# A decode step on one Trainium2 core: W_Q in four transfers of 16, 16, 32 and 64 rows instead of one of 128

## The chip, the cores and the metric

The kernel runs on one core of a Trainium2 chip. The metric is device time in microseconds from the start to the end of one execution. Before the change it is 196.24 us, the median of three runs (196.23 to 196.3).

## What is computed

The program is one decode step, for a batch of four with one token each, of a block in which attention and a gated feed-forward run in parallel on the same normalised input:

```python
x  = A_x                                   # 4 x 1 x 512, bf16
xn = _layernorm(x)
# A: 32 query heads, 8 KV heads, head size 128, only the last W = 4096 positions
q = xn @ wq                                # 512 x 4096
scores = einsum("bhqd,bhkd->bhqk", q, k) * Dh ** -0.5
o = einsum("bhqk,bhkd->bhqd", softmax(scores), v) @ wo     # wo is 4096 x 512
# B: gated feed-forward, F = 1792
ffn = (silu(xn @ w_gate) * (xn @ w_up)) @ w_down
return x + o + ffn
```

Keys and values are 33.5 MB each, W_Q and W_O 4 MB each, the three feed-forward matrices 1.8 MB each: 81 MB are read for a 4 KB result.

## The kernel before

Work is staged by KV head: eight passes, one for each head, over blocks of 4 MB of keys and 4 MB of values. A block has 128 partitions (the rows of on-chip memory), each with one contiguous run of 32 KB. There are two buffers for keys (KB) and two for values (VB). In a pass TensorE transposes the 128 key tiles (L416), VectorE and ScalarE copy the transposes out of PSUM (L336, L267), TensorE forms the scores (L425), VectorE takes maxima (L340), ScalarE the exponentials (L270), and TensorE sums and multiplies with the values (L521, L434).

All large loads are issued by SyncE, on one queue, in an order written out by hand in `run_sync`: W_Q, W_gate, W_up, K0, K1, V0, then alternately a key and a value block as buffers come free, then W_down and W_O in five pieces of columns. A key load from the third on waits until the transposes of an earlier block are done; a value load from the second on waits until an earlier product with the values is done. The small input x is loaded by ScalarE's queue (L257).

W_Q has no buffer of its own. It lies in the second value buffer (`WQ`, L57), 128 rows of 32 KB: row p holds rows 4p to 4p+3 of the matrix. It is loaded once, by the first instruction of `run_sync` (L237), and announces itself on the semaphore of that buffer, `d_v[1]`, by 16. The buffer's next user, V1, is loaded after a product with the values has released it.

TensorE's head (`t_head`) transposes the normalised x, waits for `d_v[1]` to reach 16 (L469) and then runs 32 matmuls over W_Q (L473); each contracts over all 128 partitions. ScalarE and VectorE copy the result out (L261, L310), TensorE transposes it (L480), and then the gate and up products follow (L487). TensorE's first pass begins when K0 has landed.

In the pass for head r the product with the values belongs to the pass before. In the first pass it runs over what the second value buffer holds then, W_Q, with its result unused, and with that it releases the buffer.

Of the kernel before, what the change touches and what calls it, by code (L numbers as in the profile page):

```python
# [10 lines left out]
def bass_parallel_sum__sliding_block_cached__swiglu_ffn__decode_kernel(  # L11
# [45 lines left out]
    WQ = VB[1][:].rearrange("p t d -> p (t d)").rearrange("p (c n) -> p c n", c=NC)  # L57
# [66 lines left out]
    def sem(name):  # L124
        return nc.alloc_semaphore(name=name)

    d_x = sem("d_x")
    d_k = [sem("d_k%d" % g) for g in range(2)]
    d_v = [sem("d_v%d" % g) for g in range(2)]
    d_wg = sem("d_wg")  # L130
# [46 lines left out]
    wq_ap = A_wq.rearrange("(p c) n -> p c n", c=NC)  # L177
# [7 lines left out]
    def kv_ap(cache, r):  # L185
        return cache[:, r, Sk - W:, :].rearrange("b (s t) d -> s b (t d)", t=NT)
# [39 lines left out]
    def run_sync(eng):  # L226
        def load_k(r):
            if r >= 2:
                eng.wait_ge(s_tr[NCH - 1], r - 1)
            eng.dma_start(KB[r % 2][:].rearrange("p t d -> p (t d)"), kv_ap(A_k_cache, r)).then_inc(d_k[r % 2], 16)  # L230

        def load_v(r):
            if r:
                eng.wait_ge(s_pv, r)
            eng.dma_start(VB[r % 2][:].rearrange("p t d -> p (t d)"), kv_ap(A_v_cache, r)).then_inc(d_v[r % 2], 16)

        eng.dma_start(WQ[:], wq_ap).then_inc(d_v[1], 16)  # L237
        eng.dma_start(WG[:], wg_ap).then_inc(d_wg, 16)
        eng.dma_start(WU[:], wu_ap).then_inc(d_wu, 16)
        load_k(0)  # L240
        load_k(1)
        load_v(0)
        for r in range(2, HKV):
            load_k(r)
            load_v(r - 1)
        load_v(HKV - 1)
        eng.dma_start(WD, wd_ap).then_inc(d_wd, 16)
        for q, (a, b) in enumerate(ROWS):
            if q == 0:
                eng.wait_ge(s_tr[NCH - 1], HKV - 1)  # L250
            eng.dma_start(WO[:, a:b, :], wo_ap[:, a:b, :]).then_inc(d_wo[q], 16)
        eng.wait_ge(s_y, 2)
        eng.dma_start(out_ap, y[:]).then_inc(d_out, 16)
        eng.wait_ge(d_out, 16)
# [140 lines left out]
    def run_tensor(eng):  # L395
# [60 lines left out]
        with nc.body("t_head", valid_engines=me):  # L456
            loc = eng.mark_branch_hint_location()
            for t, v in ((nx, 1), (odd, 0), (nk[0], 16), (nk[1], 16)):
                nc.regs_mov(t, v)
            eng.wait_ge(s_c2, 1)  # L460
            eng.wait_ge(s_xn, 1)
            for c in range(NC):
                last = eng.transpose(xT_ps[:, c * B:(c + 1) * B],  # L463
                                     xn[:].rearrange("b (p c) -> b c p", c=NC)[:, c, :], ident[0:B, 0:B])
            last.then_inc(s_xT, 1)
            eng.wait_ge(s_const, 1)
            mm(mask_ps, Lsel[:], Dsh[:])
            eng.wait_ge(s_xnT, 1)
            eng.wait_ge(d_v[1], 16)  # L469
            for c in range(NC):  # L470
                for j in range(2):
                    for k in range(4):
                        last = mm(ps_S[j][32 * k:32 * k + 32, :], XnT[:, c, :],  # L473
                                  WQ[:, c, 512 * (4 * j + k):512 * (4 * j + k) + 512],
                                  start=(c == 0), stop=(c == NC - 1), skip_group_check=True)
            last.then_inc(s_q, 1)
            eng.wait_ge(s_qs, 2)
            for j in range(2):
                for h in range(4):
                    last = eng.transpose(qT_ps[:, 4 * j + h, :], qs[:, j, 128 * h:128 * h + 128], ident[:])  # L480
            last.then_inc(s_qt, 1)
            for w, d, o, s_w in ((WG, d_wg, gate_ps, s_g), (WU, d_wu, up_ps, s_u)):
                wt = w[:].rearrange("p c (m t) -> p c t m", t=NF)
                eng.wait_ge(d, 16)
                for c in range(NC):
                    for k in range(4):
                        last = mm(o[32 * k:32 * k + 32, :].rearrange("p (t m) -> p t m", m=128), XnT[:, c, :],  # L487
                                  wt[:, c, T0[k]:T0[k] + 4, :], start=(c == 0), stop=(c == NC - 1), skip_group_check=True)
                last.then_inc(s_w, 1)
            eng.wait_ge(s_gu, 1)  # L490
            for t in range(4):
                last = eng.transpose(gT_ps[:, t, :], gu[:, 128 * t:128 * t + 128], ident[:])
            last.then_inc(s_gt, 1)
            eng.wait_ge(s_qc, 1)
            eng.wait_ge(s_guT, 1)
            nc.br("t_pass", engines=me)
# [102 lines left out]

    run_gpsimd(nc.gpsimd)  # L600
    run_sync(nc.sync)
    run_scalar(nc.scalar)
    run_vector(nc.vector)
    run_tensor(nc.tensor)


# [26 lines left out]
```

## Time and profile before

| | |
|---|---|
| median of three runs | 196.24 us |
| the profiled execution's own time | 196.33 us |
| its span, first to last instruction | 195.0 us |
| granted TensorE clock, mean | 0.965 |
| TensorE matmul busy | 158.2 us (81%) |
| VectorE busy | 115.5 us (59%) |
| ScalarE busy | 69.2 us (35%) |
| DMA queue of SyncE and ScalarE: packets' share of 16 engines | 97.2% |
| HBM read | 81.01 MB, 415 GB/s over the span |
| W_Q, issue to landing | 12.3 us |
| a key block, issue to landing (median) | 26.3 us |

"Busy" is time in which an engine runs an instruction. The profile has a row of the DMA engines' busy share and of GB/s in forty equal slices of the span, 4.9 us each. In a view by stretches of time, a DMA packet is counted whole in the stretch in which it starts, so that a short stretch can show a share above 1.

### The profile page before, as it was taken

The numbers are of one execution on the slowest core, as the hardware profiler recorded it, in microseconds if no ns is written. First come the engines' busy times: TensorE is split into PE (matmuls) and PEld (weight loads), VectorE is DVE, ScalarE is ACT, GpSimd is POOL, SyncE is SP. The second block draws the span as 40 slices with busy tenths as digits, with TensorE's granted clock in tenths as the row PEclk, the third lists the DMA queues.
The fourth block names the chain that finished last, engine by engine and source line by source line (L and its number), as shares of the span: only waits on it lengthen the run. The fifth ranks groups of instructions, "written<-read, shape, count | busy, mean of one in ns | idle before, by whom it ended". The sixth has DMA issues, their size and how long they took to land.

```text
span 195.0 us, 6476 instructions
## 1 busy us (share of the span) xinstructions
PE 158.2 (81%) x2889; PEld 123.0 (63%) x2898; DVE 115.5 (59%) x220; ACT 69.2 (35%) x87; POOL 8.8 (5%) x26
## 2 busy tenths in 40 slices
PE   0038945998998899899989986998799849989994
PEld 0013105986787788778778865986588549866532
DVE  4832283667667586766758673667486717674402
ACT  2003100470664357056434704470466034704001
POOL 7910000000000000000000000000000000000000
PEclk9999995899999999999999999799999978999999
DMA  6999999999999999999999999999999999998991
GB/s 229 437 424 426 440 450 437 434 437 434 420 427 423 445 423 444 430 430 430 430 430 430 430 430 430 430 430 430 444 430 430 430 430 430 430 437 376 431 401 70
DMA packets 3621, 81.09 MB, mean 416 GB/s; under 512 B 408, under 2 KB 544, under 8 KB 928
## 3 DMA queue, kind: packets, MB, share of 16 engines
q1 hardware_dynamic: 3608, 81.01, 97.2%
q8 instruction: 4, 0.07, 0.1%
q14 instruction: 1, 0.01, 0.0%
q10 hardware_dynamic: 8, 0.00, 0.0%
HBM read 81.01 MB, written 0.00 MB: 415 GB/s over the span
## 4 chain that ended last, share of the span: by engine, by line
PE 43%; DMA 42%; ACT 8%; DVE 3%; issue 2%; SPq 1%; DVEq 0%; ACTq 0%
DMA kbuf<-in_A_k_cache_dram 42%; PE ps_kt L416 20%; PE ps_s L425 8%; ACT kT L267 7%; PE ps_o L434 5%; PE ps_kt L442 2%; PE ps_s L538 2%; DVE mxb L340 1%; ACT p L270 1%; PE ps_s L582 1%; PE ps_kt L525 1%; PE ps_o L542 1%; PE ps_s L593 1%; DVE mx L363 1%; PE ps_s L572 0%
## 5 line engine op out<-in xcount | busy, mean ns | idle before, releaser
L416 PE MATMUL ps_kt<-ident,kbuf 128*128 128x128 bf16 x1024 | 72.9, 229 | 11.9 <-DMA kbuf<-in_A_k_cache_dram 8.1
L416 PEld LDWEIGHTS ps_kt<-ident,kbuf 128*128 128x128 bf16 x1024 | 62.8, 103 | 18.9 <-DMA kbuf<-in_A_k_cache_dram 8.5
L336 DVE COPY kT<-ps_kt 128x1024 bf16<-128x1024 bf16 x80 | 52.3, 688 | 23.2 <-PE ps_kt L416 22.6
L267 ACT COPY kT<-ps_kt 128x1024 bf16<-128x1024 bf16 x48 | 47.8, 1013 | 47.4 <-PE ps_kt L416 47.4
L270 ACT ACTIVATE p<-ps_s 128x512 bf16<-128x512 f32 x32 | 16.5, 603 | 43.8 <-PE ps_s L538 43.8
L340 DVE TENSOR_REDUCE mxb<-ps_s 128x16 f32<-128x512 f32 x32 | 22.1, 692 | 13.2 <-PE ps_s L425 11.6
L425 PE MATMUL ps_s<-qT,kT 128*128 x1024 | 29.5, 170 | 0.0
L425 PEld LDWEIGHTS ps_s<-qT,kT 128*128 128x128 bf16 x1024 | 27.9, 96 | 0.3
L434 PE MATMUL ps_o<-vbuf,p 128*32 128x256 bf16 x576 | 17.4, 273 | 0.6
L434 PEld LDWEIGHTS ps_o<-vbuf,p 128*32 128x32 bf16 x576 | 15.0, 97 | 2.1 <-issue 1.8
L538 PE MATMUL ps_s<-dsh,lsel 128*128 128x512 bf16 x36 | 9.4, 382 | 0.0
L521 PE MATMUL ps_kt<-p,ones 128*128 128x512 bf16 x27 | 7.6, 379 | 0.9 <-ACT p L270 0.2
L473 PE MATMUL ps_s<-vbuf,xnT 128*32 128x512 bf16 x32 | 3.6, 629 | 5.5 <-DMA vbuf<-in_A_wq_dram 5.5
L344 DVE TENSOR_REDUCE dsum<-ps_kt 128x16 f32<-128x512 f32 x9 | 6.2, 692 | 1.5 <-PE ps_kt L521 1.3
L350 DVE TENSOR_TENSOR oT<-ps_o,rden 128x16 f32 (+1 forms) x9 | 1.6, 175 | 8.9 <-PE ps_o L542 8.9
L525 PEld LDWEIGHTS ps_kt<-identf,mxd 128*128 128x128 f32 x9 | 1.3, 139 | 8.4 <-DVEq L366 8.4
L525 PE MATMUL ps_kt<-identf,mxd 128*128 128x128 f32 x9 | 2.9, 323 | 4.5 <-DVEq L366 4.5
L542 PEld LDWEIGHTS ps_o<-fold,o 128*128 128x128 f32 x36 | 5.4, 191 | 1.3
L463 PE MATMUL ps_s<-ident,xn 4*128 4x4 bf16 x4 | 0.3, 166 | 7.1 <-DVE xn L298 7.1
L473 PEld LDWEIGHTS ps_s<-vbuf,xnT 128*32 128x32 bf16 x32 | 1.2, 138 | 7.0 <-issue 7.0
L538 PEld LDWEIGHTS ps_s<-dsh,lsel 128*128 128x128 bf16 x36 | 2.8, 97 | 4.1 <-issue 1.9
L273 ACT COPY part<-ps_s 64x512 f32<-64x512 f32 x1 | 0.6, 580 | 12.2 <-PE ps_s L582 12.2
(94 smaller groups left out, 81.2 us busy)
## 6 DMA issues: line engine op xcount, KB each, us to landing
kbuf<-in_A_k_cache_dram SPq DMA_DIRECT2D x8, 4096.0 KB, 26.3
vbuf<-in_A_v_cache_dram SPq DMA_DIRECT2D x8, 4096.0 KB, 28.4
vbuf<-in_A_wq_dram SPq DMA_DIRECT2D x1, 4096.0 KB, 12.3
kbuf<-in_A_wo_dram SPq DMA_DIRECT2D x1, 2048.0 KB, 31.3
wg_sb<-in_B_w_gate_dram SPq DMA_DIRECT2D x1, 1792.0 KB, 16.1
wu_sb<-in_B_w_up_dram SPq DMA_DIRECT2D x1, 1792.0 KB, 19.9
wg_sb<-in_B_w_down_dram SPq DMA_DIRECT2D x1, 1792.0 KB, 27.0
kbuf<-in_A_wo_dram SPq DMA_DIRECT2D x1, 896.0 KB, 34.4
```

Of the source, the lines that this page charges most:

```text
L267: eng.copy(KT[n % 8][:], kt_ps[n % 3]).then_inc(s_ev[n], 1)
L270: eng.activation(P[:, q * TB:(q + 1) * TB, :], S_ps[q], ACT.Exp, scale=SCALE).then_inc(s_xp[q], 1)
L336: eng.tensor_copy(KT[n % 8][:], kt_ps[n % 3]).then_inc(s_ev[n], 1)
L340: eng.tensor_reduce(mxb[:, q, :], S_ps[q].rearrange("p t c -> p c t"), AX.X, ALU.max)
L344: eng.tensor_reduce(dsum[:], dn_ps[:].rearrange("p (t c) -> p c t", c=CQ), AX.X, ALU.add)
L416: last = eng.transpose(kt_ps[n % 3][:, k, :], KB[g][:, 8 * n + k, :], ident[:])
L425: last = mm(S_ps[q][:, 8 * (n % 4) + k, :], KT[n % 8][:, k, :], QT[:, bass.ds(j, 1), :, :].rearrange("p o b h -> p (o b h)"), start=(n % 4 ...
L434: last = mm(o4_ps[32 * k:32 * k + 32, :], P[:, 2 * u:2 * u + 2, :].rearrange("p t c -> p (t c)"), VB[e][:, 2 * u:2 * u + 2, :].rearrange(" ...
L521: last = mm(dn_ps[:], ones[:], P[:, q * TB:(q + 1) * TB, :].rearrange("p t c -> p (t c)"), start=(q == 0), stop=(q == NB - 1))
L525: eng.transpose(mx_ps, mxd[:], identf[:]).then_inc(s_mt, 1)
L538: mm(S_ps[q], Lsel[:], bc(Dsh[:], TB), start=False, stop=True, skip_group_check=True).then_inc(s_sh[q], 1)
L542: last = mm(ot_ps, o4[:, 128 * e:128 * e + 128], fold[:, 16 * e:16 * e + 16], start=(e == 0), stop=(e == 1), skip_group_check=True)
```

## The change

W_Q's load becomes four loads of the same rows: rows 0 to 15, 16 to 31, 32 to 63 and 64 to 127, in this order, on the same queue and ahead of everything that was behind it. The first three announce themselves on a new semaphore, `d_wq`, by 16 each; the last one announces itself on `d_v[1]` as the whole did. TensorE waits for `d_wq` to reach 48 and then, as before, for `d_v[1]` to reach 16. Nothing else is changed.

```diff
     d_x = sem("d_x")
+    d_wq = sem("d_wq")
     d_k = [sem("d_k%d" % g) for g in range(2)]
...
-        eng.dma_start(WQ[:], wq_ap).then_inc(d_v[1], 16)
+
+        for a, b in ((0, 16), (16, 32), (32, 64), (64, 128)):
+            eng.dma_start(WQ[a:b], wq_ap[a:b]).then_inc(d_wq if b < 128 else d_v[1], 16)
         eng.dma_start(WG[:], wg_ap).then_inc(d_wg, 16)
...
             eng.wait_ge(s_xnT, 1)
+            eng.wait_ge(d_wq, 48)
             eng.wait_ge(d_v[1], 16)
             for c in range(NC):
```

## The prediction

> **What bounds the kernel now.** I read the page first: the head, the slices, the queues and the chain of waits.
>
> ```profile
> span 195.0 us, 6476 instructions
> ...
> DMA  6999999999999999999999999999999999998991
> GB/s 229 437 424 426 440 450 437 434 437 434 420 427 423 445 423 444 430 430 430 430 430 430 430 430 430 430 430 430 444 430 430 430 430 430 430 437 376 431 401 70
> ...
> q1 hardware_dynamic: 3608, 81.01, 97.2%
> ...
> DMA kbuf<-in_A_k_cache_dram 42%; PE ps_kt L416 20%; PE ps_s L425 8%; ACT kT L267 7%; PE ps_o L434 5%; PE ps_kt L442 2%; PE ps_s L538 2%; DVE mxb L340 1%; ACT p L270 1%; PE ps_s L582 1%; PE ps_kt L525 1%; PE ps_o L542 1%; PE ps_s L593 1%; DVE mx L363 1%; PE ps_s L572 0%
> ```
>
> The DMA engines are full from the second slice to the last but one. SyncE's one queue moves 81 MB and takes 97.2% of what sixteen engines have. The chain gives more of the span to compute than to DMA, but it prefers whatever instruction ran last. Long stretches say it better: the last two columns are the busy share of the sixteen DMA engines and GB/s.
>
> ```profile
> 0.00:1.76 1.76, 0.00 (x0) 0.00 (x0) 0.11 (x1) 0.43 (x1) 1.23 (x11) 1.00 0.01 2
> 1.76:12.65 10.89, 0.45 (x5) 0.31 (x5) 7.64 (x14) 1.06 (x2) 7.60 (x17) 1.00 1.00 406
> 12.65:51.70 39.05, 31.66 (x436) 20.28 (x438) 19.91 (x35) 10.50 (x13) 0.00 (x0) 0.91 1.02 436
> 51.70:120.00 68.30, 61.94 (x1304) 51.98 (x1305) 46.92 (x91) 32.16 (x40) 0.00 (x0) 1.00 1.00 429
> 120.00:192.40 72.40, 63.34 (x1136) 49.89 (x1142) 40.49 (x79) 24.70 (x31) 0.00 (x0) 0.95 0.98 419
> 192.40:195.00 2.60, 0.82 (x16) 0.51 (x10) 0.41 (x1) 0.36 (x1) 0.00 (x0) 1.00 0.01 2
> ```
>
> One unbroken stream, then, from 1.76 to 192.40 us, 2.6 us before the end. PE waits for it where a pass is short of work (chain of waits, start and duration), and the last matmuls wait for W_O's last row:
>
> ```profile
> 2.12 29.19 DMA kbuf<-in_A_k_cache_dram
> 94.89 25.30 DMA kbuf<-in_A_k_cache_dram
> 131.68 27.39 DMA kbuf<-in_A_k_cache_dram
> ...
> 191.86 1.11 PEld L593 LDWEIGHTS ps_s<-kbuf,oP 128*32 128x32 bf16 x20 [0.21 <-DMA kbuf<-in_A_wo_dram]
> ```
>
> K blocks that are issued at 94.89 and 131.68 land 25 to 27 us later because that much is queued ahead of them. So a microsecond that the stream loses at its head, where W_Q lies, is lost at the end; nothing behind it has slack to give back.
>
> **The change part by part.** The edited issue is the first on SyncE (timeline, start and duration):
>
> ```profile
> 0.73 0.57 ACTq L257 DMA_DIRECT2D x_sb<-in_A_x_dram  x1
> 0.73 0.41 SPq L237 DMA_DIRECT2D vbuf<-in_A_wq_dram  x1
> 1.20 0.41 SPq L238 DMA_DIRECT2D wg_sb<-in_B_w_gate_dram  x1
> 1.66 0.42 SPq L239 DMA_DIRECT2D wu_sb<-in_B_w_up_dram  x1
> ...
> 156.46 2.33 SPq L251 DMA_DIRECT2D kbuf<-in_A_wo_dram  x5
> ```
>
> *Issue.* A step of SyncE is 0.47 us (0.73 to 1.20; five W_O issues in 2.33), whatever the size. Three more make 1.41 us. W_gate, W_up, K0, K1 and V0 are issued that much later: W_gate at 2.61 instead of 1.20. The engines have W_Q to move until 12.65 at least, so this is hidden, by some 9 us. Without that cover it would cost 1.41.
>
> *The wait.* PE gets a wait for 48 on the new semaphore ahead of the old one. Queued behind it are the 32 Q matmuls, then gate and up; ScalarE and VectorE wait for those. The three early parts are queued ahead of the fourth, whose wait was there already, so it adds nothing but one satisfied wait. No part is used earlier than before: every Q matmul contracts over all 128 rows. And this prologue has room:
>
> ```profile
> 13.12 3.60 PE L473 MATMUL ps_s<-vbuf,xnT 128*32 128x512 bf16 x32 [5.50 <-DMA vbuf<-in_A_wq_dram]
> ...
> 29.27 0.18 DVE L329 COPY guT<-ps_kt 128x64 bf16<-128x64 bf16 x1
> 31.36 4.72 PEld L416 LDWEIGHTS ps_kt<-ident,kbuf 128*128 128x128 bf16 x46 [2.57 <-DMA kbuf<-in_A_k_cache_dram]
> ```
>
> It ends at 29.45, and PE then waits for K0. A late W_Q makes W_gate, W_up and K0 late by the same amount, so this order stays.
>
> *Completions.* Three more transfers end. Where W_gate follows W_Q the share below is 1.00 over 4.25 us; half of its last digit is 0.02 us for one seam. Three are 0.06 us at most; I take 0.06.
>
> *The move itself* decides. Rates again, cut where packets start: a window counts those that start in it.
>
> ```profile
> 1.76:2.61 0.85, 0.00 (x0) 0.00 (x0) 0.02 (x1) 0.85 (x1) 0.58 (x5) 1.00 2.14 618
> 2.61:3.60 0.99, 0.00 (x0) 0.00 (x0) 0.84 (x3) 0.01 (x1) 0.73 (x4) 1.00 0.00 0
> 3.60:4.20 0.60, 0.00 (x0) 0.00 (x0) 0.53 (x2) 0.00 (x0) 0.44 (x1) 1.00 2.05 874
> 4.20:12.10 7.90, 0.45 (x5) 0.31 (x5) 6.26 (x11) 0.20 (x1) 5.86 (x9) 1.00 0.92 398
> 12.10:16.35 4.25, 3.23 (x32) 1.24 (x32) 0.00 (x0) 0.00 (x0) 0.00 (x0) 1.00 1.00 428
> ```
>
> A row of W_Q is 32 KB, moved as one packet. 618 GB/s for 0.85 us is 0.525 MB, sixteen rows: the first round, one row for each engine, 2.14 x 0.85 x 16 / 16 = 1.82 us each. The next sixteen start from 3.60 on and take 1.23. The six rounds after that take 0.92 x 7.90 x 16 / 96 = 1.21 us a row, 27 GB/s for an engine. Eight rounds are 9.7 us.
>
> All of this is with transfers over 128 rows, where each engine feeds eight rows that no other engine feeds. After the change sixteen engines feed rows 0 to 15, then 16 to 31, then 32 to 63, then 64 to 127. Only one transfer in the trace has several engines feed neighbouring rows: x, four rows of 1 KB. Its first, second and fourth row (in the 1.74 window other packets are mixed in):
>
> ```profile
> 1.69:1.71 0.02, 0.00 (x0) 0.00 (x0) 0.00 (x0) 0.02 (x1) 0.02 (x1) 1.00 0.14 51
> 1.71:1.73 0.02, 0.00 (x0) 0.00 (x0) 0.00 (x0) 0.02 (x1) 0.02 (x2) 1.00 0.24 51
> ...
> 2.22:2.24 0.02, 0.00 (x0) 0.00 (x0) 0.00 (x0) 0.02 (x1) 0.00 (x0) 1.00 0.14 51
> ```
>
> 51 GB/s for 20 ns is one row; its time is share x 20 x 16: 45 ns for the first, which starts by itself, 77 for the second, which overlaps its neighbours, 45 for the fourth, alone again. Rows of one group of four that arrive together take 1.7 times as long: they seem to share a way into memory that one engine nearly fills. It is a small sample, but the only row on the question.
>
> Bounds for the four parts, at 1.21 us a row. Nothing shared: 1, 1, 2 and 4 rounds, 9.7 us, no loss. Rate in proportion to the rows reached: each part takes as long as the whole, 4 x 9.7 = 38.8, a loss of 29.1. Between them I go by x. A group of four takes one engine's 27 GB/s:
> - rows 0 to 15: four engines to a group, 4 x 1.21 = 4.84 us; rows 16 to 31 the same;
> - rows 32 to 63: two rows an engine, two engines to a group, 2 x 2 x 1.21 = 4.84;
> - rows 64 to 127: four rows an engine. If groups of four are all separate, 4.84; if half of the rows get half of the rate, 9.7. I take 9.7, since the trace never shows eight rows being given more than one engine's 27 GB/s.
>
> 3 x 4.84 + 9.7 = 24.2 us, 14.5 more than now. Sixteen engines work their queues in the same order, so I don't let parts overlap.
>
> [...]
>
> **The sum** is made against the profiled execution, 196.33 us (span 195.0 and 1.3 around it), 0.09 over the median of 196.24: 196.33 + 14.5 + 0.06 + 0 for issues and wait = 210.9, **210.8** against the median. Own range of this case: 206.0 (last part 4.84, a gain of 4.84 on the sum) to 212.0 (a row's 1.21 more, engines out of step).
>
> **Rivals.**
> *Nothing is shared, no change.* Each engine moves its rows at 1.21 us wherever they lie. The head can't start sooner by more than 0.06: x, with four rows, has its first packet at 1.70, W_Q with 128 at 1.76. Against that stand 0.06 of seams: 196.2. For it: sixteen engines stay busy. Against it: x's second row.
>
> *The start gets shorter, faster.* The place is the first round: rows start between 1.76 and 2.61, and none of the second round before 3.60. If transfers of one row per engine start every engine at 1.70 and at the steady 1.21, the second round begins at 2.91 rather than 3.60 to 4.20, worth up to 1.29. Half of that, 0.65, gives 195.6. It decides if nothing is shared and the spread comes from laying out 128 rows. Against it: x gave each engine one row only, and its fourth still started at 2.22, 0.5 late; and the issue takes 0.41 for 128 rows, 0.57 for x's four.
>
> *Rows keep their engines.* If an engine is tied to rows, a part of 16 rows uses few engines, nothing is shared, and the engines of rows 64 to 127 stand idle until the fourth issue, 1.41 late. A K block has landed only when the last engine has, so the end moves by 1.41: 197.7. [...]
>
> *In proportion to rows.* 196.24 + 29.1 = 225.3. For it only that no row excludes it; x's four rows got more than a thirty-second of the rate.
>
> **How the numbers follow.** A measurement of this kernel tells 0.2%, 0.39 us, from no change. Chances: the forecast 0.53, in proportion 0.03, rows keep engines 0.10 (these three slower, 0.66); nothing shared 0.19 (same); shorter start 0.15 (faster). Time 210.8. Range 196.0 to 212.0: it takes in the forecast, the lag and no change, 0.82, and leaves out the faster case and the proportional one. The forecast's own range stands above; between it and 197.7 I expect little.
>
> **What would show it.** SyncE issues L237's successor four times at 0.47 us. In the slices GB/s falls to about 110, 110, 220 and 220 until some 26 us, then returns to 430; the single rows of the first two parts take near 4.8 us. The Q matmuls start near 27.6 instead of 13.12, PE's first transposes near 45.9 instead of 31.36, the stream ends near 207, and everything behind keeps its distances. If the first slices show 430 and L473 starts near 13, sharing is wrong and a start rival holds; half the engines' rate for 1.4 us would be the tied rows. If the Q matmuls come late but the end doesn't, it is my unbroken stream that is wrong.

## The result

The changed kernel takes 210.4 us (median, 210.17 to 210.7) against 196.24 before (196.16 to 196.41): 1.0715 times as long, 95% interval 1.0703 to 1.0727. The prediction was 210.8. The profiled execution took 210.4 us, with a span of 208.9.

The page of the changed kernel, its head, slices and queue; the slices are 5.2 us each here:

```profile
span 208.9 us, 6479 instructions
...
DMA  9969699999999999999999999999999999999992
GB/s 126 176 144 257 144 395 464 402 445 455 402 405 480 411 402 472 427 402 433 452 420 408 471 427 408 458 439 402 427 458 420 408 471 427 408 452 401 434 392 105
...
q1 hardware_dynamic: 3656, 81.01, 97.6%
```

The DMA engines still count as full, 97.6% of their time against 97.2% before. But in the first five slices they move 126 to 257 GB/s where they moved 424 to 440 from the second slice on. The packets are not fewer (3656 for 3608); they take longer. "Busy" says here that an engine has a packet under way, not at what rate its bytes flow.

W_Q and what follows it, cut where the rounds of packets start (last two columns: share of sixteen engines, GB/s). Every window but the last holds sixteen rows of 32 KB, one for each engine; the last is W_gate:

```profile
1.76:4.99 3.23, 0.00 (x0) 0.00 (x0) 2.51 (x5) 0.85 (x1) 2.34 (x10) 1.00 1.11 162
4.99:9.49 4.50, 0.46 (x5) 0.31 (x5) 3.26 (x6) 0.20 (x1) 4.16 (x6) 1.00 1.01 117
9.49:12.84 3.35, 0.00 (x0) 0.00 (x0) 2.18 (x5) 0.00 (x0) 1.37 (x3) 1.00 0.94 157
12.84:15.41 2.57, 0.00 (x0) 0.00 (x0) 0.00 (x0) 0.00 (x0) 0.00 (x0) 1.00 1.00 204
15.41:17.84 2.43, 0.00 (x0) 0.00 (x0) 0.00 (x0) 0.00 (x0) 0.00 (x0) 1.00 1.01 216
17.84:20.41 2.57, 0.00 (x0) 0.00 (x0) 0.00 (x0) 0.00 (x0) 0.00 (x0) 1.00 1.00 204
...
22.98:25.55 2.57, 0.00 (x0) 0.00 (x0) 0.00 (x0) 0.00 (x0) 0.00 (x0) 1.00 1.00 204
25.55:30.42 4.87, 3.25 (x32) 1.27 (x32) 0.00 (x0) 0.00 (x0) 0.00 (x0) 1.00 0.98 377
```

The second part (rows 16 to 31) needs 4.50 us for a round that took 1.21 before. The third part is the next two windows, the fourth the four from 15.41 to 25.55, at about 2.57 a round, 204 GB/s. W_Q's packets are through at 25.55 instead of 12.10, and W_gate needs 4.87 instead of 4.25: its first sixteen rows start beside the last ones of W_Q and take nearly a microsecond each (a share of 2.06 over the 0.48 us in which they start), where a row of W_gate took 0.53 before (4.25 us for eight rows an engine).

Behind that next to nothing changes. The rest of the stream of the changed kernel, then the timeline where the Q matmuls and the first pass start:

```profile
30.42:206.35 175.93, 153.65 (x2846) 120.53 (x2853) 107.28 (x204) 67.36 (x84) 0.00 (x0) 0.96 1.00 427
206.35:208.90 2.55, 0.80 (x16) 0.45 (x10) 0.41 (x1) 0.36 (x1) 0.00 (x0) 1.00 0.01 2
```

```profile
0.73 1.91 SPq L240 DMA_DIRECT2D vbuf<-in_A_wq_dram  x4
...
27.17 3.61 PE L477 MATMUL ps_s<-vbuf,xnT 128*32 128x512 bf16 x32 [19.27 <-DMA vbuf<-in_A_wq_dram]
...
45.21 3.06 PE L419 MATMUL ps_kt<-ident,kbuf 128*128 128x128 bf16 x27 [2.14 <-DMA kbuf<-in_A_k_cache_dram]
```

From W_gate's last packets to the end of the stream it is 175.93 us; before, from 16.35 to 192.40, 176.05. The Q matmuls start 14.05 us later (27.17 for 13.12), the first pass 13.85 later (45.21 for 31.36), the stream ends 13.95 later, the span is 13.9 longer.

### The profile page after: what moved, and what is told of

Read it like the earlier page. It is cut to its first block, busy times and chain, and to the rows that moved or that the text cites. A ratio compares the mean times of both kernels' runs of the same rounds, so it can differ in the third digit from the quotient of the medians.

```text
span 208.9 us, 6479 instructions
## 1 busy us (share of the span) xinstructions
PE 158.2 (76%) x2889; PEld 122.6 (59%) x2898; DVE 115.8 (55%) x220; ACT 69.2 (33%) x87; POOL 9.1 (4%) x26
## 3 DMA queue, kind: packets, MB, share of 16 engines
q1 hardware_dynamic: 3656, 81.01, 97.6%
## 4 chain that ended last, share of the span: by engine, by line
DMA 45%; PE 40%; ACT 8%; DVE 3%; issue 2%; SPq 1%; DVEq 0%; ACTq 0%
DMA kbuf<-in_A_k_cache_dram 45%; PE ps_kt L419 20%; PE ps_s L428 8%; ACT kT L270 7%; PE ps_o L437 5%; PE ps_kt L445 2%; PE ps_s L542 2%; DVE mxb L343 1%; ACT p L273 1%; SPq L240 1%; PE ps_s L586 1%; PE ps_o L546 1%; PE ps_kt L529 1%; PE ps_s L597 1%; DVE mx L366 0%
## 5 line engine op out<-in xcount | busy, mean ns | idle before, releaser
L264 ACT CAST kT<-ps_s 128x512 bf16<-128x512 f32 x1 | 0.6, 585 | 25.2 <-PE ps_s L477 25.2
```

## The experiments

But for the two kernels on what the head is worth, the experiments change only how W_Q is loaded and the count that TensorE waits for. Diffs are against the kernel before; they show the lines that stand in the place of W_Q's one load, without the new semaphore and the count. The theory on trial, S, is an assumption that the rounds of the changed kernel allow (4.50 us for 16 neighbouring rows, about 2.57 in the parts of 32 and 64): the 128 rows have sixteen ways in, rows of a group of four share one, with the group 32 rows on, and engines that feed the same way at once slow each other. Rivals: N, each extra transfer costs; P, the rate goes by the number of rows; G, groups of four that are all separate.

### Four transfers by columns

```diff
+        wq_row = wq_ap.rearrange("p c n -> p (c n)")
+        WQ_row = WQ[:].rearrange("p c n -> p (c n)")
+        for a, b in ((0, 2048), (2048, 4096), (4096, 8192), (8192, 16384)):
+            eng.dma_start(WQ_row[:, a:b], wq_row[:, a:b]).then_inc(d_wq if b < 16384 else d_v[1], 16)
```

> W_Q in four transfers again, in the same shares (1/8, 1/8, 1/4, 1/2) and with the same waits, but cut by columns: each covers all 128 rows. Theory S, shared ways: rows of a group of four, and the group 32 rows above it, come in through one way, and engines that feed the same way at once slow each other; here each engine feeds rows of its own, so no loss: 196.2 us, within 0.4. Theory N, the number of transfers: three more transfers cost what they cost in the changed kernel, 14 us: 210. If the start gets shorter because the first transfer is small, a little under 196.2, at best 195.6.

Measured: 196.46 us against 196.33 on the same chip, ratio 1.0025 (1.0004 to 1.0046); four of its twelve runs took 197.4 to 198.3 us, and no trace says why. Four transfers in the same shares cost at most half a per cent, so N falls, and there is no gain either. The window to the end of W_Q's packets and W_gate's:

```profile
1.76:12.17 10.41, 0.45 (x5) 0.31 (x5) 7.94 (x14) 1.06 (x2) 7.87 (x17) 1.00 1.00 403
12.17:16.46 4.29, 3.44 (x32) 1.27 (x32) 0.00 (x0) 0.00 (x0) 0.00 (x0) 1.00 1.01 428
```

W_Q's packets give way to W_gate's at 12.17, before at 12.10: a first transfer of few bytes doesn't shorten the head.

### Two halves, blocks of 16, every eighth row

```diff
+        for a, b in ((0, 64), (64, 128)):
+            eng.dma_start(WQ[a:b], wq_ap[a:b]).then_inc(d_wq if b < 128 else d_v[1], 16)
```

> W_Q in two transfers of 64 rows. Theory S: each half reaches 8 of 16 ways, two engines to a way; the changed kernel's rows took 2.575 us so, eight rounds are 20.6 instead of 9.7, a loss of 10.9: 207.1 us. Theory N: one extra transfer, a third of 14: 200.9. Theory G, groups of four that are all separate: no loss, 196.2. Theory P, rate in proportion to rows: twice the time, 19.4 for 9.7: 205.9.

Measured: 206.85 us, ratio 1.053 (1.0515 to 1.0546).

```diff
+        for a in range(0, 128, 16):
+            eng.dma_start(WQ[a:a + 16], wq_ap[a:a + 16]).then_inc(d_wq if a < 112 else d_v[1], 16)
```

> W_Q in eight transfers of 16 neighbouring rows. Theory S: four engines to a way throughout; the changed kernel's second part took 4.50 us a round, eight are 36.0, a loss of 26.3: 222.5 us, or 0.9 less if the first round is as short as there. Theory N: seven extra transfers at 4.7: 229. Theory P: eight times 9.7: 264.

Measured: 222.94 us, ratio 1.1347 (1.133 to 1.1363).

```diff
+        for a in range(8):
+            eng.dma_start(WQ[a:a + 121:8], wq_ap[a:a + 121:8]).then_inc(d_wq if a < 7 else d_v[1], 16)
```

> W_Q in eight transfers of 16 rows as in the run with blocks, but each takes every eighth row. Theory S: two rows of a transfer share a way (p and p+32), 2.575 us a round, eight are 20.6, a loss of 10.9: 207.1 us. Theory G, only rows of one group of four share: no loss, 196.2. If any transfer of 16 rows is slow, whichever rows: the same as the run with blocks, 222. Theory N: 229.

Measured: 206.95 us, ratio 1.0532 (1.0517 to 1.0547). One round of sixteen rows from each of the three, in this order:

```profile
3.94:6.50 2.56, 0.00 (x0) 0.00 (x0) 2.06 (x5) 0.20 (x1) 2.18 (x5) 1.00 1.01 205
```

```profile
28.08:32.66 4.58, 0.00 (x0) 0.00 (x0) 0.00 (x0) 0.00 (x0) 0.00 (x0) 1.00 1.01 115
```

```profile
16.51:19.08 2.57, 0.00 (x0) 0.00 (x0) 0.00 (x0) 0.00 (x0) 0.00 (x0) 1.00 1.00 204
```

The forecasts of S were 207.1, 222.5 and 207.1. The last two kernels have the same eight transfers of sixteen rows and the same bytes, and differ by 16 us: it matters which rows go together. Every eighth row, two to a way if p and p + 32 share one, costs the same as a half of 64 rows. G, for which rows eight apart never meet, falls with 206.95 for its 196.2; P falls with 222.94 for its 264.

### A middle part that meets all ways

```diff
+        for a, b in ((0, 32), (32, 96), (96, 128)):
+            eng.dma_start(WQ[a:b], wq_ap[a:b]).then_inc(d_wq if b < 128 else d_v[1], 16)
```

> W_Q in three transfers: rows 0 to 31, 32 to 95, 96 to 127. Theory S: the outer two have two engines to a way, two rows an engine at 2.58; the middle one has the same 64 rows a transfer as the halves, but its rows reach all 16 ways, one engine each, four rows at 1.21: 5.15 + 4.85 + 5.15 = 15.2 instead of 9.7, a loss of 5.5: 201.8 us. If a transfer of 64 rows is slow whichever rows they are: 5.15 + 10.3 + 5.15, a loss of 10.9: 207.1. Theory N: two more transfers: 205.6.

Measured: 201.93 us, ratio 1.0279 (1.0252 to 1.0306). A round of the first part, two of the middle part and the last of the third:

```profile
3.67:6.25 2.58, 0.00 (x0) 0.00 (x0) 2.01 (x6) 0.20 (x1) 2.11 (x5) 1.00 1.00 203
8.37:9.58 1.21, 0.00 (x0) 0.00 (x0) 1.21 (x1) 0.00 (x0) 1.21 (x3) 1.00 1.01 433
9.58:10.80 1.22, 0.00 (x0) 0.00 (x0) 1.19 (x3) 0.00 (x0) 0.87 (x1) 1.00 1.00 430
14.06:16.60 2.54, 0.00 (x0) 0.00 (x0) 0.00 (x0) 0.00 (x0) 0.00 (x0) 1.00 1.01 206
```

This is the plainest of them. Rows 0 to 63 move at 205 GB/s, rows 32 to 95, as many and as contiguous, at 430. So the rate goes neither by the number of rows nor by the size of a transfer: rows 0 to 31 share with rows 32 to 63, but rows 32 to 63 don't share with rows 64 to 95.

In all these kernels row p of W_Q goes to partition p, so the ways could also lie at the other end, at the rows' addresses in HBM. No run moves the same rows to other partitions, but W_gate speaks against that end. Its rows are 14 KB (1792 KB over 128 partitions). Which of them move together is not shown; if they are four apart, each engine keeping a group of four, they lie 56 KB apart in HBM, closer than the 128 KB within which four rows of W_Q share; yet W_gate moves at 428 GB/s over all 128 partitions. That is an argument, not a test.

### Both halves at once, from two queues

The first line is SyncE's, the others are ScalarE's:

```diff
+        eng.dma_start(WQ[0:64], wq_ap[0:64]).then_inc(d_wq, 16)
...
         eng.dma_start(X[:], x_ap).then_inc(d_x, 16)
+        eng.dma_start(WQ[64:128], wq_ap[64:128]).then_inc(d_v[1], 16)
```

> W_Q's rows 0 to 63 issued by SyncE and rows 64 to 127 by ScalarE right after x, so that both halves are in flight together. Theory S with engines in step (all on the lower half, then all on the upper): as with two halves one after the other, 207. Theory S with the halves truly side by side (an engine's two rows under way at once, all 16 ways fed): the loss goes, 196.3, or up to 0.6 more for ScalarE's later issue. [...]

Measured: 206.51 us, ratio 1.0518 (1.05 to 1.0535), 0.34 us under the halves one after the other. The stretch of W_Q:

```profile
2.10:6.43 4.33, 0.00 (x0) 0.00 (x0) 3.52 (x8) 1.27 (x2) 3.26 (x10) 1.00 1.11 242
6.43:11.37 4.94, 0.46 (x5) 0.31 (x5) 4.09 (x6) 0.00 (x0) 4.28 (x5) 1.00 1.00 212
11.37:18.60 7.23, 0.00 (x0) 0.00 (x0) 0.33 (x3) 0.00 (x0) 0.00 (x0) 1.00 1.01 218
```

It never comes near 430 GB/s, though together the two transfers cover all rows. That is what S gives for engines that work in step, all on one half and then all on the other; a second queue doesn't put the halves side by side here.

### Is the head really worth its full time at the end?

One kernel brings 2 MB less of W_Q, one brings 2 MB more, each over all 128 rows. The first leaves out half of W_Q, reads the other half twice and zeroes the rest of the buffer; in the second SyncE waits for the extra transfer ahead of the output.

```diff
+        eng.dma_start(WQ[:, 0:2], wq_ap[:, 0:2]).then_inc(d_v[1], 16)
...
-                                  WQ[:, c, 512 * (4 * j + k):512 * (4 * j + k) + 512],
+                                  WQ[:, c % 2, 512 * (4 * j + k):512 * (4 * j + k) + 512],
...
         eng.memset(OP[:], 0.0)
+        eng.memset(WQ[:, 2:4, :], 0.0)
```

> One transfer over 128 rows, but only the first half of each row (2 MB instead of 4); the Q matmuls read that half twice, so this kernel leaves out half of W_Q, and the rest of the buffer is zeroed by GpSimd. If the stream is unbroken from its head to its end, four rounds of 1.21 us less at the head are 4.85 less at the end: 191.4 us. If something behind the head has slack or bounds by itself (the rival that the head is hidden), less is gained, down to nothing: 196.3.

Measured: 192.53 us, ratio 0.9805 (0.9788 to 0.9821), a gain of 3.8 instead of 4.85. Its timeline (GpSimd, VectorE, TensorE) and two windows of it show where the rest went:

```profile
10.38 6.93 POOL L224 MEMSET vbuf<- 128x8192 bf16 x1
...
7.30 10.21 DVE L307 COPY i<-identf 16x16 f32<-16x16 f32 x2
...
18.88 1.03 PE L483 MATMUL ps_kt<-ident,kT 128*128 128x128 bf16 x8 [7.03 <-DVE kT L313]
...
31.48 0.81 PE L419 MATMUL ps_kt<-ident,kbuf 128*128 128x128 bf16 x6 [1.07 <-DVEq L333]
...
44.00:46.00 2.00, 1.93 (x52) 1.36 (x49) 1.75 (x3) 0.00 (x0) 0.00 (x0) 1.00 1.03 352
46.00:48.00 2.00, 1.46 (x42) 1.21 (x45) 1.26 (x6) 0.00 (x0) 0.00 (x0) 1.00 0.84 328
```

VectorE's two 16x16 copies, which took 3.35 us before, lasted until the added zeroing was over (17.51 us, its end at 17.31), the Q path waited 7 us for it, and the first pass waited for that and not for K0. Buffers were given back no sooner for the shorter head (the third key block was issued at 43.66 us, before at 43.51), and the stream ran thin at 44 to 48 us, at 352 and 328 GB/s. So the cover that the prediction relied on, a prologue that ends before K0 lands, was gone there, by the experiment's own doing; that this makes up the whole missing microsecond is not shown. The other direction has no such side effect:

```diff
         eng.dma_start(WQ[:], wq_ap).then_inc(d_v[1], 16)
+        eng.dma_start(XTRA[:], wq_ap[:, 0:2]).then_inc(d_wq, 16)
```

> W_Q in one transfer as before, followed by one more transfer over 128 rows that brings 2 MB of W_Q into a buffer that nothing reads. No row is shared, nothing waits for it but SyncE ahead of the output. If the stream is unbroken to its end, four rows an engine at 1.21 us are 4.85 more: 201.2 us. If the head were hidden in part, less, down to 196.3.

Measured: 201.36 us, ratio 1.0255 (1.0237 to 1.0273): 5.1 us more on the medians for a transfer that takes 4.86 in the stream:

```profile
12.07:16.93 4.86, 3.60 (x32) 1.24 (x32) 0.24 (x2) 0.24 (x1) 0.00 (x0) 1.00 1.01 432
```

What the head loses here, the end loses.

### Where the simple sharing is not enough

```diff
+        for a, b in ((0, 16), (16, 128)):
+            eng.dma_start(WQ[a:b], wq_ap[a:b]).then_inc(d_wq if b < 128 else d_v[1], 16)
```

> W_Q in two transfers, of 16 and of 112 rows. Theory S worked out round by round, an engine's seven rows in order, engines on one way slowing each other by the measured prices (alone 1.21 us, two 2.58, three some 3.6, four 4.55): 15.9 us instead of 9.7, a loss of 6.2: 202.5 us, or 0.9 less for a short first round. Theory N: 4.7 for one more transfer: 200.9. A slow transfer of 16 rows and an undisturbed one of 112: 4.5 and 7 x 1.21, a loss of 3.3: 199.6. Theory P: 9.7 more, 206.

Measured: 205.64 us, ratio 1.0475 (1.0458 to 1.0493), 3 us above S and nearest to P, which had fallen elsewhere. (S's price for three engines on a way, 3.6 us, is an estimate between the prices for two and four, 2.58 and 4.55; no run shows it.) The time alone says little: that S stops at W_Q's last row. By S, engines that have run out of W_Q go on to W_gate and then share ways with the last rows of W_Q. Carried on by the same prices through W_gate, W_up, K0 and K1, S comes to some 205.2 us here, and to 206.8, 202.0 and 203.2 for the three kernels below; these are estimates from those prices, with an engine's rows taken in order; no run shows which engine took a row.

The rows say more. By S, most ways are fed by one engine at any time in the transfer of 112 rows, and twelve of the second round's sixteen rows should take 1.21 us. Yet no round is near that. The second, whole and cut in two, and the fourth:

```profile
8.24:10.52 2.28, 0.00 (x0) 0.00 (x0) 2.28 (x1) 0.00 (x0) 2.28 (x3) 1.00 1.00 230
...
8.24:8.65 0.41, 0.00 (x0) 0.00 (x0) 0.41 (x1) 0.00 (x0) 0.41 (x1) 1.00 5.55 1279
8.65:10.52 1.87, 0.00 (x0) 0.00 (x0) 1.87 (x1) 0.00 (x0) 1.87 (x3) 1.00 0.00 0
...
12.32:13.98 1.66, 0.00 (x0) 0.00 (x0) 0.00 (x0) 0.00 (x0) 0.00 (x0) 1.00 1.04 316
```

Sixteen rows start within 0.41 us, and for 1.87 us after that no engine is free to start another; W_gate is not under way yet.

Either an engine is slow on a way that it doesn't feed in a transfer over 128 rows (X), or many such ways together are (L), or engines on a shared way hold up others (spilling). Three kernels tell these apart.

```diff
+        for a in range(12):
+            eng.dma_start(WQ[a:128:12], wq_ap[a:128:12]).then_inc(d_wq if a < 11 else d_v[1], 16)
```

> W_Q in twelve transfers of 11 or 10 rows, 12 rows apart, so that no two rows of a transfer share a way. Ten engines then move twelve rows each, one moves eight, five move none. This asks what one engine by itself gets on a way that isn't the one it feeds in a transfer over 128 rows, since the run with 16 and 112 rows was 3 us slower than theory S said. Theory S alone: 1.21 us a row, twelve are 14.6, a loss of 4.9: 201.2 us. Theory X, a strange way costs by itself: rows at 1.67 us (the shortest in that run) or more, 20 us, a loss of 10.3 or more: 206.7 or above.

Measured: 207.69 us, ratio 1.0574 (1.0557 to 1.0592). The time alone would speak for X, but the rows don't. Two transfers of eleven rows in the middle of it, and a stretch near its end:

```profile
6.63:7.88 1.25, 0.46 (x5) 0.31 (x5) 0.43 (x3) 0.00 (x0) 1.10 (x3) 1.00 0.67 288
7.88:9.10 1.22, 0.00 (x1) 0.00 (x0) 1.22 (x1) 0.00 (x0) 1.22 (x1) 1.00 0.69 295
...
16.00:18.61 2.61, 0.00 (x0) 0.00 (x0) 0.00 (x0) 0.00 (x0) 0.00 (x0) 1.00 1.05 219
```

Eleven of sixteen engines are busy, a share of 0.69, at 0.69 x 1.22 x 16 / 11 = 1.22 us a row, where 1.21 is the steady figure before: if these ways are strange to their engines, that costs nothing. X falls. The loss comes later, when W_gate's packets run beside the last transfers (219 GB/s), and S carried on through W_gate foretells most of it (206.8).

```diff
+        for a in range(9):
+            eng.dma_start(WQ[a:128:9], wq_ap[a:128:9]).then_inc(d_wq if a < 8 else d_v[1], 16)
```

> W_Q in nine transfers of 15 or 14 rows, nine rows apart; no two rows of a transfer share a way, and 14 or 15 engines work. In the run with steps of 12 eleven engines kept 1.21 us a row for as long as nothing else was under way, and were slowed to 2.5 once W_gate's rows ran beside them. Theory S alone: 1.21 us a row, nine rows are 10.9, a loss of 1.2: 197.5 us, somewhat more if W_gate's first rows, moved by engines that have run out of W_Q, meet the last ones. Theory L, strange ways together take less than 430 GB/s (314, the best of the run with 16 and 112 rows): 1.65 us a row from the first full round, 14.9, a loss of 5.2: 201.5 us.

Measured: 202.84 us, ratio 1.033 (1.0278 to 1.0382), which neither number foretold; S carried on through W_gate gives 202.0. The second transfer of 15 rows, one of 14, and the last one with W_gate and the next loads beside it:

```profile
4.30:5.50 1.20, 0.00 (x0) 0.00 (x0) 0.98 (x3) 0.04 (x1) 0.82 (x3) 1.00 1.00 410
9.24:10.49 1.25, 0.00 (x0) 0.00 (x0) 1.25 (x1) 0.00 (x0) 1.25 (x3) 1.00 0.91 367
13.06:16.30 3.24, 0.00 (x0) 0.00 (x0) 0.00 (x0) 0.00 (x0) 0.00 (x0) 1.00 0.91 199
```

Fifteen rows, by S on fifteen ways, move at 410 GB/s, so L falls too. In the last transfer, beside W_gate, the rate drops to 199.

```diff
+        for a in range(7):
+            eng.dma_start(WQ[a:a + 106:7], wq_ap[a:a + 106:7]).then_inc(d_wq, 16)
+        eng.dma_start(WQ[112:128], wq_ap[112:128]).then_inc(d_v[1], 16)
```

> W_Q in seven transfers of 16 rows, seven rows apart, and one of rows 112 to 127. In each of the seven one or two ways are fed by two engines, all others by one. Theory S alone, worked out row by row: a row at 1.21, or 2.58 where shared, 14.8 us in all, a loss of 5.1: 201.4 us, with rows of both lengths side by side. Theory S with spilling, an engine on a shared way also holds up engines whose own way is free: all rows of the seven near 2.58, 7 x 2.58 + 4.55 = 22.6, a loss of 12.9: 209.2 us.

Measured: 205.66 us, ratio 1.0454 (1.042 to 1.0488), between the two, and 2.5 above S carried on through W_gate (203.2). Windows of 2 us in each of which sixteen rows start, those of the second, third, fifth and seventh transfer, then the third transfer cut in two:

```profile
3.50:5.50 2.00, 0.00 (x0) 0.00 (x0) 1.77 (x4) 0.00 (x0) 1.43 (x5) 1.00 1.08 262
5.50:7.50 2.00, 0.46 (x5) 0.31 (x5) 1.21 (x5) 0.20 (x1) 1.84 (x5) 1.00 1.13 262
...
9.50:11.50 2.00, 0.00 (x0) 0.00 (x0) 1.77 (x5) 0.00 (x0) 0.96 (x2) 1.00 0.82 262
...
13.50:15.50 2.00, 0.00 (x0) 0.00 (x0) 0.00 (x0) 0.00 (x0) 0.00 (x0) 1.00 1.12 262
...
5.94:6.90 0.96, 0.00 (x0) 0.01 (x1) 0.76 (x2) 0.00 (x0) 0.96 (x3) 1.00 2.35 546
6.90:8.19 1.29, 0.46 (x5) 0.31 (x5) 0.96 (x2) 0.00 (x0) 1.13 (x2) 1.00 0.00 0
```

Share x 2 us is a row's mean time: 2.16, 2.26, 1.64 and 2.24 us. By S, four of sixteen engines share a way in these transfers, and two in the fifth. If only they were slow, with the others at 1.21 and these at 2.58, the mean would be 1.55, and 1.38 in the fifth. The last two lines show it without a mean: sixteen rows start within 0.96 us, and for 1.29 us after that no engine starts another, although by S twelve have a way of their own, on which a row takes 1.21. So, by S, a shared way also slows engines that have their own; how much differs from transfer to transfer (means of 1.64 to 2.26 us a row), and by which path no run shows.

## Why the prediction was right, step by step

- **The bound.** An unbroken stream whose head is paid for at the end: right. The stretch behind W_gate took 175.93 us for 176.05, and 2 MB more at the head cost 5.1 us for 4.85. The half of W_Q taken away gave 3.8, since there the prologue became late; the order "prologue, then K0" is a condition, as the prediction had it.
- **Issue and wait.** Four issues in 1.91 us, hidden, no cost: right. That a step of SyncE is 0.47 us whatever the size was read too widely: K0 and K1, in the same trace, take 0.63 each. TensorE's 19.27 us of idle time are W_Q's landing, not the new wait.
- **Seams.** 0.06 taken. Four transfers by columns cost 0.13 us on the medians and W_Q's packets ended 0.07 later; too small to tell.
- **The move itself.** Right in kind and near in size, 24.2 us forecast, 23.8 measured from 1.76 to 25.55, but by terms that were off in both directions. First part 4.84 forecast, 3.23 until the next one starts; second 4.84, 4.50; third 4.84, 5.92 (3.35 and 2.57); fourth 9.7, 10.14. By S, two engines on a way paid 2.57 us a row rather than 2.42, four paid 4.50 rather than 4.84. The first is 1.61 below the forecast and the third 1.08 above; that these nearly cancel is luck. Left out was W_gate's slow first round, 0.62 us, and the baseline was 0.64 too low (9.7 for a head that takes 10.34 from 1.76 to 12.10); that these cancel is luck as well. In all 14.5 was forecast, and 13.9 came in the span, 14.2 on the medians.
- **The fourth part** was the open choice, 4.84 or 9.7. It took 10.14, and the middle part of 64 rows, with, by S, all ways in reach, 1.21 us a round: that points to the +32 sharing as what made it slow.
- **The row it rested on was weak.** The prediction read sharing out of one row of x that took 77 ns instead of 45. In the changed kernel three of x's rows start within 50 ns of each other, in windows of 20 ns in which two and one of these packets of 1 KB start:

```profile
1.69:1.71 0.02, 0.00 (x0) 0.00 (x0) 0.00 (x0) 0.02 (x1) 0.02 (x1) 1.00 0.28 102
1.71:1.73 0.02, 0.00 (x0) 0.00 (x0) 0.00 (x0) 0.02 (x1) 0.02 (x2) 1.00 0.14 51
```

0.28 x 20 x 16 / 2 is 45 ns each, 0.14 again 45: side by side and not slowed. So the inference was no evidence, and as far as the traces went by then, the kind of loss was a guess that came true.
- **Rivals.** Nothing shared and a shorter start: no. The engines did start closer together, sixteen rows between 1.76 and 2.10 instead of 2.61, but the first packet is where it was. Rows tied to engines: no. The first sixteen rows all start by 2.10 and no other row before 4.99, so sixteen engines moved one each. In proportion to rows: no, 222.94 for eight blocks of sixteen where it gives 264.
- **Not foreseen** was that parts hold each other up beyond the shared ways. In this change all engines of a part share alike, so it didn't show.

## What to carry to other kernels

Cut a load by columns, not by rows: four pieces over all 128 rows cost half a per cent at most here, the same four shares of the rows cost 14 us of 196. If rows must be cut, look at which rows travel together: here 32 to 95 went at full rate (430 GB/s), 0 to 63 at half (205), 16 neighbours at a quarter (115), and a transfer with, by S, a single shared way took 1.64 us a row on the mean instead of 1.21. And a DMA share of 1.00 isn't bandwidth (it stood at 204 GB/s and at 428 here); read GB/s beside it, above all where the stream is the bound and each lost microsecond is paid for at the end.

## What the runs showed that was not expected

- Spilling, above: rows of a transfer at 1.6 to 2.3 us on the mean where, by S, twelve or fourteen of sixteen engines had a way of their own.
- By S, four engines on a way got more in all than one did: 4 x 32 KB in 4.50 us is 29 GB/s, one engine 27, two engines 25.5.
- Two 16x16 copies on VectorE lasted 10.21 us while GpSimd zeroed memory, and ended with its last memset (10.38 + 6.93 = 17.31 us, the copies 17.51). In the kernel before the same two end 0.2 us after GpSimd's last memset too, after 3.35 us.
- SyncE's issue of a transfer isn't 0.47 us for every one: twelve transfers of 11 or 10 rows were issued in 9.50 us, 0.79 each:

```profile
0.74 9.50 SPq L240 DMA_DIRECT2D vbuf<-in_A_wq_dram  x12
```
